# Second-product groups two by two, the seven products reordered, and a second PSUM buffer for X

## The chip, the cores and the metric

The kernel runs on one core of one Trainium2 chip. The metric is the time of one execution in microseconds on the device; the kernel before has a median of 1407.38 us over three runs (1406.71 to 1407.70). All arithmetic of the matmuls is done on a pair of reduced-precision float32 tiles, a high part and a low part (`hi`/`lo`, `xh`/`xl`, `hh`/`hl`), so every product of two matrices is three matmuls: high by high, high by low, low by high.

## The reference

Attention over local windows, then a mixture of eight experts with ReLU, then a layer with a rational activation. Only the middle part is touched here:

```python
P = np.exp(logits - logits.max())          # x @ w_gate, 1536 x 8
for _ in range(8):
    P /= P.sum(1, keepdims=True) + 1e-09
    P /= P.sum(0, keepdims=True) + 1e-09
    P *= N / E
for e in range(E):
    h = np.maximum(x @ w1[e], 0.0)         # 1536 x 512 by 512 x 1024
    ye = h @ w2[e]                         # 1024 x 512
    out += P[:, e:e + 1] * ye
```

## The kernel before, in words

The experts' hidden columns are cut into 16 units of 512. The first unit is worked out in the ordinary way, overlapped with the attention. The other 15 units are 30 subunits `v` of 256 columns, and each is done by `block(v, j)` for two halves `j` of the tokens (768 each): 60 blocks. A block forms the first product (weights 256 x 512 by 512 x 768 tokens) by Strassen's method in Winograd's form: seven products of quarters instead of eight, each of six matmuls of 384 columns (lines 1003 to 1005). The results are collected in three PSUM tiles: X (one bank, accumulated by four products in turn, and read after each of them), Y (two products) and Z (one product). `s1`, `s2`, `s3` are SBUF tiles: ScalarE copies X into one (lines 1018, 1023, 1029), VectorE adds Y or Z (lines 1026, 1032, 1039). `hidden` then makes the ReLU on ScalarE (`hh`, line 1011) and the low part on VectorE (`hl`, line 1012). That of `s2` is put off (`late`) until after product 0 of the next block.

The second product of a block is six groups of 128 tokens (`g2w`): each is six matmuls of 512 columns (lines 176 to 178) into one of three `psm` tiles, `p_v`, which VectorE then scales by the gate and adds to `accs` (line 1064; line 1059 for the first expert). The groups of a block are appended to the queue `g2q` after product 6, each due two ticks later, and issued in the next block.

The order is written out by hand: instructions go to each engine's queue in the order in which the Python code emits them, and each engine works its queue in order. Between the products stand the calls of `step`, here called places 0 to 5 of a block (after products 0, 1, 3, 4, 5, 6). `step` calls `tick`, which counts a point, may run one job, issues one group if the first in the queue is due, and from v = 2 on runs one of the `cv` jobs. The latter turn 64 pieces of the last layer's weights from float64 to float32 in five jobs each: a load by DMA (`cv_load`), `cv_round` (two VectorE instructions, then two on GpSimd, lines 782 to 789), `cv_join` (lines 795 and 798, which need GpSimd's result), `cv_add` (lines 803 and 806), and `cv_store` by DMA. The list `jobs` holds first the normalisation of P, due at points 4, 6, 8, ... 22: `sk_max_b`, `sk_first`, then eight `sk_step`s. Each `sk_step` is a matmul `csp <- cs` (line 738, column sums), VectorE's column scaling (lines 739 to 742) and, but for the last, row sums and the next `cs` (lines 730 to 734). The rule for jobs in `tick` is

```python
if g2q and g2q[0][0] <= point[0] or not g2q:
    run_job()
```

so a job waits while the first group in the queue is not yet due. At v = 0 the steps also run `rest`, the last two pieces of the token operands. After each product `sub_weights` gives GpSimd a piece of the next subunit's weights (at j = 0 `w_sums`, four sums of 128 x 256, lines 924 to 927; `w_op` and `w2_op`, lines 112 and 113, split into high and low), and SP the DMAs of the weights (`sa`, `sb`). SP also issues the `cv` loads and stores.

PSUM's eight banks in this stage: three for `psm`, one each for X, Y and Z (`psx`), two for `psb` (tag "g"), which holds the small tiles of the normalisation and is unused from v = 2 on.

Of the kernel before, what the change touches and what calls it, by code (L numbers as in the profile page):

```python
# [10 lines left out]
F32 = mybir.dt.float32  # L11
# [11 lines left out]
def kernel(  # L23
# [14 lines left out]
    nc = tc.nc  # L38
    B, H, S, D = q.shape
    NT, DM = out.shape  # L40
    NE, _, FE = w1.shape
    F2 = w_out.shape[0]
    P = 128
# [632 lines left out]
    psx = wctx.enter_context(tc.tile_pool(name="psx", bufs=1, space=PSUM))  # L676
    psb = wctx.enter_context(tc.tile_pool(name="psb", bufs=2, space=PSUM))
# [141 lines left out]
    point = [0]  # L819
    g2q = []  # L820

    def run_job():
        if jobs and jobs[0][0] <= point[0]:
            jobs.pop(0)[1]()

    def tick(cv=False):

        point[0] += 1
        if g2q and g2q[0][0] <= point[0] or not g2q:
            run_job()  # L830
        if g2q and g2q[0][0] <= point[0]:
            g2q.pop(0)[1]()
        if cv and cvjobs:
            cvjobs.pop(0)()

# [75 lines left out]

    wop = {}
    wS = {}
    OPS = ["A11", "S2", "A12", "S3", "S1", "A22", "S4"]

    def w_quarter(v, name):
        st = sg["v", v, 1]
        f, k = int(name[1]) - 1, int(name[2]) - 1
        return st[:, 2 * k:2 * k + 2, f * P:(f + 1) * P]
# [10 lines left out]
    def w_op(v, i):  # L930
        name = OPS[i]
        src = w_quarter(v, name) if name[0] == "A" else wS[v][:, int(name[1]) - 1]
        t = wpool.tile([P, 2, 2, P], F32R, tag="w1", name=f"w{name}_{v}")
        split(t[:, 0], t[:, 1], src, v == 0)
        wop[v, i] = t
# [8 lines left out]
    def sub_weights(v, j, i):  # L944

        n = v + 1
        if j == 0:
            if v == 0:
                if i < 2:
                    w2_op(0, i)  # L950
                elif i == 2:
                    dma_sub(1, 2)
                    w_sums(1)
                elif i != 4:
                    w_op(1, {3: 0, 5: 1, 6: 2}[i])
            elif n < NSUB:
                if i == 0:
                    w_sums(n)
                elif i % 2:
                    w_op(n, i // 2)  # L960
            elif i == 5:
                split_w(U1, 1, 0)
        elif n < NSUB:
            if i < 4:
                w_op(n, 3 + i)
            elif i < 6:
                w2_op(n, i - 4)
            if i == 3:
                dma_sub(n + 1, 1) if n + 1 < NSUB else dma_w(U1, 1, 0)
            if i == 5:  # L970
                dma_sub(n + 1, 2) if n + 1 < NSUB else dma_w(U1, 1, 1)
        else:
            if i in (0, 2, 4):
                split_w(U1, 1, 1 + i // 2)
            if i in (1, 5):
                dma_w(U1, 2, i // 4)

    late = []

    def step(v):  # L980
        tick(v > 1)
        if rest and point[0] % 2:
            rest.pop(0)()

    def block(v, j):

        n = NW
        o1, o2, ot = j * HT, j * HT + n, j * n
        X, Y, Z = (psx.tile([P, 512], F32, tag=t, name=f"{t}_{v}_{j}")[:, :n] for t in ("X", "Y", "Z"))
        s1, s2, s3 = (vpool.tile([P, n], F32, tag=t, name=f"{t}_{v}_{j}") for t in ("s1", "s2", "s3"))  # L990

        def xs(k, o):
            return lambda t: (xh[:, 2 * k + t, o:o + n], xl[:, 2 * k + t, o:o + n])

        def tt(i):
            return lambda t: (th[i][:, t, ot:ot + n], tl[i][:, t, ot:ot + n])

        def product(i, ps, get, start):
            w = wop[v, i]
            go = {} if start else {"skip_group_check": True}  # L1000
            for t in range(2):
                mh, ml = get(t)
                nc.tensor.matmul(ps, lhsT=w[:, 0, t], rhs=mh, start=start and t == 0, stop=False, **go)  # L1003
                nc.tensor.matmul(ps, lhsT=w[:, 0, t], rhs=ml, start=False, stop=False, **go)  # L1004
                nc.tensor.matmul(ps, lhsT=w[:, 1, t], rhs=mh, start=False, stop=t == 1, **go)  # L1005
            sub_weights(v, j, i)

        def hidden(c, half, src):
            hh = hp["pool"].tile([P, n], F32R, tag="hh", name=f"hh_v{v}_{j}_{c}{half}")
            hl = hp["pool"].tile([P, n], F32R, tag="hl", name=f"hl_v{v}_{j}_{c}{half}")  # L1010
            nc.scalar.activation(hh, src, AF.Relu)  # L1011
            nc.vector.scalar_tensor_tensor(  # L1012
                out=hl, in0=src, scalar=0.0, in1=hh.bitcast(F32), op0=ALU.max, op1=ALU.subtract
            )
            ht["v", v, j, c, half] = (hh, hl)

        product(0, X, xs(0, o1), True)
        nc.scalar.copy(s1, X)  # L1018
        while late:
            late.pop()()  # L1020
        step(v)
        product(1, X, tt(0), False)
        nc.scalar.copy(s2, X)
        step(v)
        product(2, Z, xs(1, o1), True)
        nc.vector.tensor_add(s1, s1, Z)  # L1026
        hidden(0, 0, s1)
        product(3, X, tt(1), False)
        nc.scalar.copy(s3, X)
        step(v)  # L1030
        product(4, Y, xs(0, o2), True)
        nc.vector.tensor_add(s3, s3, Y)  # L1032
        hidden(1, 1, s3)
        step(v)
        product(5, X, tt(2), False)
        hidden(1, 0, X)
        step(v)
        product(6, Y, xs(1, o2), False)
        nc.vector.tensor_add(s2, s2, Y)
        late.append(lambda: hidden(0, 1, s2))  # L1040
        for half in range(2):
            for t in range(n // P):
                g2q.append((point[0] + 2, lambda half=half, t=t: g2w(v, j, half, t)))
        step(v)

    def g2w(v, j, half, t):
        g = (j * HT + half * NW) // P + t
        u = UW + v // 2
        ps = psm.tile([P, 512], F32, tag="mm", name=f"p2_v{v}_{g}")
        o = t * P  # L1050

        def get(c):
            hh, hl = ht["v", v, j, c, half]
            return (hh[:, o:o + P], hl[:, o:o + P]), wt["v", v, c]

        mm3(ps, 2, get)
        a, e = acc[g], u // UPE
        if e == 0:
            nc.vector.tensor_add(a, a, ps)
        else:  # L1060
            if u == UPE and v % 2 == 0:
                assert not jobs
                acc_scale(g)
            nc.vector.scalar_tensor_tensor(  # L1064
                out=a, in0=ps, scalar=Pt[:, g, e:e + 1], in1=a, op0=ALU.mult, op1=ALU.add
            )
        if v == NSUB - 1:
            jobs.append((point[0] + 2, lambda: to_x(g)))

    def unit(u, blocks, delay, extra=None):  # L1070
        for b, (t0, n) in enumerate(blocks):
            for c in range(NCH):
                weights(u, b, len(blocks), c, True)
                g1(u, t0, n, c)
                weights(u, b, len(blocks), c, False)
                if c == NCH - 1:
                    for t in range(n // P):
                        g2q.append((point[0] + 2 + delay, lambda t0=t0, t=t: g2(u, t0, t)))
                tick()
                if extra:  # L1080
                    extra(b, c)
# [20 lines left out]
    for m in range(len(mains)):  # L1102
# [4 lines left out]
        if m == g1s - 1:  # L1107
            assert not plan
            for i in range(2, len(OPS)):
                w_op(0, i)  # L1110
# [3 lines left out]
    for v in range(NSUB):  # L1114
        for j in range(2):
            block(v, j)
    assert not cvjobs
    late.pop()()
    while g2q or jobs:
        tick()  # L1120
# [45 lines left out]
```

## Time and profile before

| | |
|---|---|
| median of three runs | 1407.38 us (1406.71 to 1407.70) |
| span of the profiled execution | 1408.2 us |
| TensorE matmuls busy | 1371.1 us (97%) |
| VectorE busy | 1083.5 us (77%) |
| GpSimd busy | 830.9 us (59%) |
| ScalarE busy | 503.9 us (36%) |
| mean granted TensorE clock | 0.995 |
| the 60 blocks | from 177 to 1125 us |

The profile is one execution of its own. Its span, first instruction to last, is 0.8 us above the median of the runs; no other time of that execution is listed. A busy TensorE is not TensorE at its peak: matmuls are pipelined, and the distance from the start of one matmul to the start of the next tells its cost better than the duration in its row. Of an engine that is not the bottleneck, idle time costs nothing by itself. A granted clock of 1.00 is 2.4 GHz, one of 0.5 is 1.2 GHz.

### The profile page before, as it was taken

To read this page: it belongs to the slowest core of one execution; us is meant where nothing else is said; L and a number is where in the kernel's file an instruction comes from. 1 tells how busy PE (TensorE), PEld (TensorE's weight loads), DVE (VectorE), ACT (ScalarE), POOL (GpSimd) and SP (SyncE) were. 2 spreads that over 40 slices of the span, in tenths; PEclk is the share of its full clock that TensorE was granted. 3 is DMA by queue.
4 is the path that set the end of the run, shared out by engine and by line. 5 is a ranking of instruction groups with operands and counts; after the bars stand their busy time and mean duration, and the time that the engine had idled before them with its cause. 6 is when DMAs were issued, how large, how long until landed. Compare 5 with 4: busy or idle time off the path is not lost.

```text
span 1408.2 us, 19502 instructions
## 1 busy us (share of the span) xinstructions
PE 1371.1 (97%) x7207; PEld 1209.2 (86%) x7207; DVE 1083.5 (77%) x1856; ACT 503.9 (36%) x1106; POOL 830.9 (59%) x1034
## 2 busy tenths in 40 slices
PE   6799989999999999999999999999999999999998
PEld 5788879988998989888988889888998888888886
DVE  6876867677777777676777777676777589999996
ACT  5665422321222222222222122112221268777673
POOL 5631584576767676676776776666776134545541
PEclk9999999999999999999999999999999999999999
DMA  9531021122112122122212122212221100100002
GB/s 240 141 99 29 0 60 38 54 64 64 60 57 77 55 79 64 55 62 64 64 53 79 54 78 64 64 54 64 64 69 62 39 31 15 46 30 31 31 7 83
DMA packets 90366, 86.08 MB, mean 61 GB/s; under 512 B 22944, under 2 KB 70048, under 8 KB 90272
## 3 DMA queue, kind: packets, MB, share of 16 engines
q1 hardware_dynamic: 90272, 84.84, 20.1%
q8 instruction: 57, 0.93, 0.3%
q14 instruction: 37, 0.30, 0.1%
HBM read 73.29 MB, written 11.53 MB: 60 GB/s over the span
## 4 chain that ended last, share of the span: by engine, by line
PE 62%; DVE 21%; POOL 7%; ACT 6%; DMA 2%; issue 1%; SPq 0%; ACTq 0%; DVEq 0%; POOLq 0%
PE p_v L178 10%; PE p_v L177 10%; PE p_v L176 10%; PE X L1003 5%; PE X L1004 5%; PE X L1005 5%; DVE r L216 4%; PE Y L1004 3%; PE Y L1005 2%; PE Y L1003 2%; DVE ta L219 2%; DVE ab L213 2%; DVE ab L202 2%; DVE ta L206 2%; DVE accs L248 1%; DVE ta L205 1%
## 5 line engine op out<-in xcount | busy, mean ns | idle before, releaser
L1064 DVE SCALAR_TENSOR_TENSOR accs<-p_v,Pt,accs 128x512 f32<-128x512 f32 x336 | 250.3, 745 | 71.9 <-PE p_v L178 70.6
L178 PE MATMUL p_v<-w2h_v,hl_v 128*128 128x512 f32 x720 | 286.3, 398 | 0.0
L177 PE MATMUL p_v<-w2l_v,hh_v 128*128 128x512 f32 x720 | 284.7, 395 | 0.0
L176 PE MATMUL p_v<-w2h_v,hh_v 128*128 128x512 f32 x720 | 282.1, 392 | 0.0
L1011 ACT ACTIVATE hh_v<-s 128x384 fp32r<-128x384 f32 x180 | 94.8, 527 | 349.5 <-DVE s L1026 198.9
L1012 DVE SCALAR_TENSOR_TENSOR hl_v<-s,hh_v 128x384 fp32r<-128x384 f32 x180 | 131.5, 730 | 104.5 <-ACT hh_v L1011 104.5
L788 POOL TENSOR_SCALAR ce<-ce 128x256 uint32<-128x256 uint32 x64 | 69.0, 1078 | 154.3 <-DVE ce L782 154.3
L178 PEld LDWEIGHTS p_v<-w2h_v,hl_v 128*128 128x128 f32 x720 | 135.2, 188 | 28.9
L176 PEld LDWEIGHTS p_v<-w2h_v,hh_v 128*128 128x128 f32 x720 | 135.6, 188 | 17.0
L177 PEld LDWEIGHTS p_v<-w2l_v,hh_v 128*128 128x128 f32 x720 | 135.3, 188 | 16.9
L223 POOL TENSOR_TENSOR hl<-ta,hh 128x512 fp32r<-128x512 f32 (+1 forms) x52 | 63.1, 1213 | 141.4 <-ACT hh L222 130.0
L1018 ACT COPY s<-X 128x384 f32<-128x384 f32 x60 | 28.7, 478 | 250.2 <-PE X L1005 250.2
L112 POOL TENSOR_SCALAR wS<-S 128x256 fp32r<-128x256 f32 x116 | 56.0, 483 | 89.3 <-PE X L1005 87.4
L176 PE MATMUL p<-xh,w1h 128*128 128x512 f32 (+2 forms) x288 | 102.8, 357 | 0.0
L113 POOL TENSOR_TENSOR wS<-S,wS 128x256 fp32r<-128x256 f32 x120 | 96.8, 807 | 9.7
L178 PE MATMUL p<-xh,w1l 128*128 128x512 f32 (+2 forms) x288 | 101.7, 353 | 0.0
L177 PE MATMUL p<-xl,w1h 128*128 128x512 f32 (+2 forms) x288 | 101.7, 353 | 0.0
L176 PE MATMUL p<-w2h,hh 128*128 128x512 f32 x240 | 95.2, 396 | 2.4 <-DVE accs L248 2.3
L178 PE MATMUL p<-w2h,hl 128*128 128x512 f32 x240 | 94.2, 393 | 1.8 <-DVE hl L191 1.7
L177 PE MATMUL p<-w2l,hh 128*128 128x512 f32 x240 | 94.0, 392 | 0.0
L113 POOL TENSOR_TENSOR w2l_v<-sb,w2h_v 128x512 fp32r<-128x512 f32 x60 | 80.5, 1341 | 5.0
L1003 PE MATMUL Y<-xh,wS 128*128 128x384 f32 x240 | 80.2, 334 | 2.4 <-DVE s L1032 2.4
(204 smaller groups left out, 3419.8 us busy)
## 6 DMA issues: line engine op xcount, KB each, us to landing
sa<-in_moe_w_dram SPq DMA_DIRECT2D x30, 512.0 KB, 3.5
sb<-in_moe_w_dram SPq DMA_DIRECT2D x30, 512.0 KB, 3.9
cv<-in_moe_w_in_dram SPq DMA_DIRECT2D x32, 256.0 KB, 3.5
cv<-in_moe_w_out_dram SPq DMA_DIRECT2D x32, 256.0 KB, 3.2
f_in<-cf SPq DMA_DIRECT2D x32, 128.0 KB, 2.2
f_out<-cf SPq DMA_DIRECT2D x32, 128.0 KB, 1.8
s<-f_in SPq DMA_DIRECT2D x8, 512.0 KB, 3.4
s<-f_out SPq DMA_DIRECT2D x8, 512.0 KB, 3.5
```

Of the source, the lines that this page charges most:

```text
L113: (sub or nc.gpsimd).tensor_sub(lo, src, hi.bitcast(F32))
L176: nc.tensor.matmul(ps, lhsT=sh, rhs=mh, start=(i == 0), stop=False)
L177: nc.tensor.matmul(ps, lhsT=sh, rhs=ml, start=False, stop=False)
L178: nc.tensor.matmul(ps, lhsT=sl, rhs=mh, start=False, stop=(i == n_k - 1))
L223: nc.gpsimd.tensor_sub(hl[:, :n], ta, hh[:, :n].bitcast(F32))
L788: nc.gpsimd.tensor_scalar(out=e, in0=e, scalar1=896, scalar2=0, op0=ALU.subtract, op1=ALU.max)
L1003: nc.tensor.matmul(ps, lhsT=w[:, 0, t], rhs=mh, start=start and t == 0, stop=False, **go)
L1004: nc.tensor.matmul(ps, lhsT=w[:, 0, t], rhs=ml, start=False, stop=False, **go)
L1005: nc.tensor.matmul(ps, lhsT=w[:, 1, t], rhs=mh, start=False, stop=t == 1, **go)
L1011: nc.scalar.activation(hh, src, AF.Relu)
L1012: nc.vector.scalar_tensor_tensor(out=hl, in0=src, scalar=0.0, in1=hh.bitcast(F32), op0=ALU.max, op1=ALU.subtract)
L1064: nc.vector.scalar_tensor_tensor(out=a, in0=ps, scalar=Pt[:, g, e:e + 1], in1=a, op0=ALU.mult, op1=ALU.add)
```

## The change

The seven products of a block come in another order, and so do the weight operands (`OPS`): S1 and S3 change places as well as A12 and S2. Products go to X, Z, X, Y, X, X, Y instead of X, X, Z, X, Y, X, Y. There are still six places in a block, now after products 0, 1, 2, 3, 4 and 6. `tick` takes a number of groups: two at the places 1, 3 and 4, none at 0, 2 and 5. From v = 2 on X comes from the two `psb` buffers. The sum and `hidden` of s1 now stand ahead of the copy of s2, and the sum of s3 directly behind the copy of s3.

```diff
-    def tick(cv=False):
+    def tick(cv=False, groups=1):
 
         point[0] += 1
         if g2q and g2q[0][0] <= point[0] or not g2q:
             run_job()
-        if g2q and g2q[0][0] <= point[0]:
-            g2q.pop(0)[1]()
+        for _ in range(groups):
+            if g2q and g2q[0][0] <= point[0]:
+                g2q.pop(0)[1]()
...
-    OPS = ["A11", "S2", "A12", "S3", "S1", "A22", "S4"]
+    OPS = ["A11", "A12", "S2", "S1", "S3", "A22", "S4"]
...
-    def step(v):
-        tick(v > 1)
+    def step(v, i):
+        tick(v > 1, 2 if i in (1, 3, 4) else 0)
...
-        X, Y, Z = (psx.tile([P, 512], F32, tag=t, name=f"{t}_{v}_{j}")[:, :n] for t in ("X", "Y", "Z"))
+        pools = (psb if v > 1 else psx, psx, psx)
+        X, Y, Z = (
+            p.tile([P, 512], F32, tag="g" if p is psb else t, name=f"{t}_{v}_{j}")[:, :n]
+            for p, t in zip(pools, ("X", "Y", "Z"))
+        )
...
-        step(v)
-        product(1, X, tt(0), False)
-        nc.scalar.copy(s2, X)
-        step(v)
-        product(2, Z, xs(1, o1), True)
+        step(v, 0)
+        product(1, Z, xs(1, o1), True)
         nc.vector.tensor_add(s1, s1, Z)
         hidden(0, 0, s1)
-        product(3, X, tt(1), False)
+        step(v, 1)
+        product(2, X, tt(0), False)
+        nc.scalar.copy(s2, X)
+        step(v, 2)
+        product(3, Y, xs(0, o2), True)
+        step(v, 3)
+        product(4, X, tt(1), False)
         nc.scalar.copy(s3, X)
-        step(v)
-        product(4, Y, xs(0, o2), True)
         nc.vector.tensor_add(s3, s3, Y)
         hidden(1, 1, s3)
-        step(v)
+        step(v, 4)
         product(5, X, tt(2), False)
         hidden(1, 0, X)
-        step(v)
         product(6, Y, xs(1, o2), False)
         nc.vector.tensor_add(s2, s2, Y)
         late.append(lambda: hidden(0, 1, s2))
         for half in range(2):
             for t in range(n // P):
                 g2q.append((point[0] + 2, lambda half=half, t=t: g2w(v, j, half, t)))
-        step(v)
+        step(v, 5)
```

## Rows read from the trace of the kernel before

**Rows 1.** Busy time by stretch; after the engines: granted clock, DMA share, GB/s.

```profile
68.70:72.20 3.50, 2.89 (x9) 2.53 (x10) 3.40 (x7) 1.77 (x5) 1.07 (x2) 0.51 0.69 183
188.20:195.10 6.90, 6.31 (x17) 5.30 (x18) 3.46 (x11) 1.28 (x3) 5.85 (x10) 0.51 0.10 37
...
300.00:1100.00 800.00, 796.05 (x3966) 714.12 (x3965) 586.45 (x1021) 167.23 (x357) 543.76 (x676) 1.00 0.21 64
```

**Rows 2.** Waits of TensorE's matmuls, 170 to 1125 us: total, times, longest.

```profile
PE X L1003 <- POOL wS L112: 4.4, 4, 1.4
PE Y L1003 <- DVE s L1032: 2.4, 1, 2.4
PE X L1003 <- DVE hl_v L1012: 0.7, 1, 0.7
PE X L1003 <- ACT s L1029: 0.6, 2, 0.3
PE X L1003 <- ACT s L1018: 0.6, 1, 0.6
```

**Rows 3.** Timelines of VectorE, ScalarE and TensorE around one late product 5.

```profile
434.02 0.29 DVE L782 TENSOR_SCALAR ce<-cv 128x256 uint32<-128x256 uint32 x1 [2.91 <-DMA cv<-in_moe_w_in_dram]
...
436.68 0.43 DVE L795 SCALAR_TENSOR_TENSOR cs<-cv,ce 128x256 uint32<-128x256 uint32 x1 [0.80 <-POOL ce L789]
...
440.36 0.54 DVE L1026 TENSOR_TENSOR s<-s,Z 128x384 f32<-128x384 f32 x1
...
440.94 0.52 ACT L1011 ACTIVATE hh_v<-s 128x384 fp32r<-128x384 f32 x1 [6.57 <-DVE s L1026]
441.37 0.46 ACT L1029 COPY s<-X 128x384 f32<-128x384 f32 x1
...
435.03 0.33 PE L1003 MATMUL Z<-xh,wA 128*128 128x384 f32 x1
...
436.07 0.33 PE L1003 MATMUL X<-th,wS 128*128 128x384 f32 x1
...
440.70 0.40 PE L178 MATMUL p_v<-w2h_v,hl_v 128*128 128x512 f32 x1
441.97 0.41 PE L1003 MATMUL X<-th,wA 128*128 128x384 f32 x1 [0.88 <-POOL wS L112]
```

**Rows 4.** Timeline of TensorE: the first matmuls of two blocks that follow each other.

```profile
241.16 0.33 PE L1003 MATMUL X<-xh,wA 128*128 128x384 f32 x1
...
256.80 0.33 PE L1003 MATMUL X<-xh,wA 128*128 128x384 f32 x1
```

**Rows 5.** Timelines: the normalisation's sums, and a block's start.

```profile
203.68 0.16 DVE L739 TENSOR_SCALAR cr<-csp 128x8 f32<-128x8 f32 x1
...
206.58 0.34 DVE L734 TENSOR_REDUCE cs<-Pt 128x8 f32<-128x96 f32 x1
...
220.25 0.16 DVE L739 TENSOR_SCALAR cr<-csp 128x8 f32<-128x8 f32 x1
...
222.23 0.36 DVE L734 TENSOR_REDUCE cs<-Pt 128x8 f32<-128x96 f32 x1
...
225.01 0.34 PE L1003 MATMUL X<-xh,wA 128*128 128x384 f32 x1
...
226.71 0.53 ACT L1011 ACTIVATE hh_v<-s 128x384 fp32r<-128x384 f32 x1
...
228.51 0.28 PE L738 MATMUL csp<-cs,ones 128*128 128x8 f32 x2
...
228.83 0.17 DVE L739 TENSOR_SCALAR cr<-csp 128x8 f32<-128x8 f32 x1 [0.15 <-PE csp L738]
```

**Rows 6.** Groups of instructions, 300 to 1130 us: busy, mean ns, idle before them.

```profile
L1064 DVE SCALAR_TENSOR_TENSOR accs<-p_v,Pt,accs 128x512 f32<-128x512 f32 x317 | 236.1, 745 | 69.7 <-PE p_v L178 69.0
...
L924 POOL TENSOR_TENSOR S<-sa 128x256 f32<-128x256 f32 x25 | 22.8, 912 | 0.8
```

**Rows 7.** Timeline of TensorE ahead of the half-clock stretch at 68.7 us.

```profile
66.06 0.70 PE L456 MATMUL sc<-accs,qz 128*128 128x120 f32 x4 [1.49 <-DVE a L463]
```

## The prediction

> **What bounds the kernel now.** I read the windows first: from 300 to 1100 us TensorE is busy 796.05 of 800 us at the full clock, VectorE 586 and GpSimd 544 [rows 1]. So in the long middle the sixty blocks go at TensorE's own pace, and another engine counts only where TensorE waits for it. The timeline gives that pace: a first product took 1.04 us (435.03 to 436.07) [rows 3], and a block 15.64 us (241.16 to 256.80) [rows 4], so a group takes (15.64 - 7 x 1.04) / 6 = 1.39 us. The change leaves out and adds no matmul; it can only move waits. The list of what TensorE waited for, 170 to 1125 us, is therefore the whole budget [rows 2]:
> - 3.7 us in block 0: 2.4 for the sum s3 += Y, 0.7 for the second reader of X, 0.6 for the copy s1.
> - 4.4 + 0.6 = 5.0 us in six waits of product 5 (writes X, L1003), once in ten blocks. The timeline shows one: the group's last matmul starts at 440.70 and would be over at 440.93; product 5 starts at 441.97, 1.04 us late where the row shows 0.88 [rows 3]. With 0.16 more on each, the six cost 6.0 us.
>
> A third loss stands in no list of waits: from 188.2 to 195.1 us, right behind block 0's waits, the granted clock is 0.51, which is the 1.2 GHz level [rows 1]. 6.9 us at half pace, less 0.7 us of waiting within, cost about 3 us.
>
> **The six waits of product 5: minus 6.0 us.** In the one shown, the releaser named is GpSimd, but its weights were not what was late: VectorE waited 2.91 us for a cv load, so s1 += Z began at 440.36; ScalarE's ReLU of s1 at 440.94; behind it in ScalarE's queue the copy of s3 at 441.37, which product 5 needs [rows 3]. Z was complete at 436.07, so the sum was 3.9 us late. In the new order Z is product 1 (its end: 2.1 us into a block), the copy behind the ReLU is that of s2, and the product that needs it is number 4, at 9.7 us (two products, two groups, two products, two groups: 4 x 1.04 + 4 x 1.39). With the sum 3.9 us late it begins at 6.4, the ReLU ends near 7.0 and the copy near 7.5: 2 us to spare. Product 5 now needs only the s3 copy, with two groups (2.78 us) for a 0.46 us copy. I take the whole 6.0; the lower bound is 5.0, as listed.
>
> **New waits from block 4 on: plus 1 us.** What is late next is s3 += Y, for product 6 at 14.6 us. The cv jobs still come one at a place, but between places 1 and 2 VectorE now has no other work, so a join that follows its round there must wait for GpSimd. In the instance of before, the round's start, GpSimd's two steps and the join's start took 434.02 to 436.68 = 2.66 us, and from the join to the sum behind it, with one group's addition between, 3.68 us [rows 3]. In the new order the second group's product is complete at 4.9 us, so the round starts near 6.1; join at 8.8; 3.68 us and one more addition of 0.745 us [rows 6] later, at 13.2, s3 += Y starts, and ends at 13.8. That leaves 0.8 us. This meeting comes in one block of five (five cv jobs against six places), 11 times. Were GpSimd first to finish the four weight sums of a new subunit (0.91 us each [rows 6], 3.6 us), which stand in every second block, product 6 would wait about 2 us in some 5 of these: plus 10. The sums of before were over before the round came, so I take 1 us; bounds 0 and 10. DMAs: SP's order is kept, except that cv's store and load of place 4 now pass ahead of the sb load issued at product 5, which spares them its wait; the price is nothing where the sb load's tile is used a block later. PSUM: two groups in a row need two of three psm buffers; the additions are 0.745 us against 1.39 a group, so none is short.
>
> **The second buffer of X: nothing from block 4 on, plus 0.5 us before.** Up to v = 1 X keeps one buffer, and product 0 now follows product 5 after one product (1.04 us), where a group, a product and a group lay. ReLU and subtraction of X take about 0.3 + 0.5 + 0.55 us: some 0.25 us late at two borders. Bounds 0 and 1.
>
> **Block 0: minus 0.7 us.** No group is due there, so products stand back to back, and its 3.7 us of waits [rows 2] only change places: the s2 copy now stands behind the ReLU of s1, the s3 copy behind a cast of the last operands. What sets the block's end is in both orders VectorE's chain: the last operands, s3 += Y, the two subtractions. I give it the last of the waits, 0.7; bounds minus 1.5 and plus 1.
>
> **The row and column sums: plus 9.6 us.** This is what the diff doesn't show. A job runs in a tick only when the first group in the queue is due (or none is queued). Until now the queue's old last group was still due at place 5. With two groups at places 1, 3 and 4 the queue is empty before place 5; the six new ones are appended there, due two ticks on. So place 5 runs no job, and the jobs due at points 6, 12 and 18 run at 7, 13 and 19, place 0 of blocks 1 to 3. The next ones, due at 8, 14 and 20, run at place 1: only product 1 (1.04 us) lies between. Each job's matmul csp needs cs from the job ahead, and stands in TensorE's queue ahead of the groups.
> How long cs takes: cr starts 0.32 us after csp (228.51, 228.83), and from cr to the end of cs VectorE takes 2.34 us (220.25 to 222.59) up to 3.24 us (203.68 to 206.92) [rows 5]. Ahead of it in VectorE's queue stands now hl of the former block's s2, whose ReLU starts 1.70 us after product 0 starts (225.01, 226.71) and takes 0.53 us [rows 5]; hl takes 0.5 more, so cr starts at 2.7 us and cs ends at 5.1 to 6.0. TensorE stands ready at 2.2 us: a wait of 2.9 to 3.8 us, 3.3 in the middle. For the pair at 13 and 14 and that at 19 and 20, that is 6.6. At points 7 and 8 the first job is sk_first (a copy, an exponential, a row sum): I give that pair a little less, 3.0. Sum 9.6; above 11.4, below 3 x 1.5 = 4.5, were hl not ahead. Until now at least a group and a product lay between two jobs, and TensorE waited nowhere.
> The Trainium skill ("SBUF — State Buffer", "Who interferes with whom") says that VectorE instructions with two SBUF inputs, or in a two-port mode, are held up by GpSimd; 2.34 against 3.24 us for the same nine instructions agrees, and by it GpSimd's weight splitting would make each of the three waits one of 3.8, 11.4 in all.
>
> **The clock: plus 1.5 us.** Another half-clock stretch, 68.7 to 72.2 us [rows 1], follows a wait of 1.49 us at 66.06 [rows 7] and lasts 3.5 us. A wait of 3.3 us is longer than the 2.4 of block 0. I take three stretches of the short kind (half of 3.5 lost, less what falls into waiting: 1.5 each) in place of the one that costs 3. Bounds: none (minus 3) and the long kind behind each wait (3 x 3 - 3 = plus 6).
>
> **Sum.** -6.0 + 1 + 0.5 - 0.7 + 9.6 + 1.5 = +5.9 us. The profiled span is 1408.2, 0.8 above the median of the runs; on the median 1407.4 + 5.9 = 1413.3. A measurement of this kernel tells 0.2% (2.8 us) from no change.
>
> **Rivals.**
> - *Faster: the pairs of sums cost little.* If cs comes when hl isn't ahead (1.5 us each) and no half-clock stretch remains: -6.0 - 0.7 + 4.5 + 0.5 - 3 = -4.7, 1402.7. With those 3 us of clock back and the other terms as in the sum, it decides from waits of under 1.8 us each (-6.0 + 1 + 0.5 - 0.7 - 3 + 3 x 1.8 = -2.8). For it: the six waits surely go. Against: hl is issued ahead of the job in the text of the block. 0.25, of which 0.15 below 1404.6 and 0.10 within 0.2%.
> - *The clock falls for long at every wait:* plus 6 instead of 1.5: 1417.8. For it: 6.9 us behind block 0's waits. Against: the stretch at 68.7 us is half as long. The Trainium skill ("TensorE: Matmul & The Clock Gate", "HAM oscillation") speaks against a change that makes TensorE idle between bursts: each idle stretch brings the low clock again. That the low clock follows waits, the trace shows; by the rule the time is this rival's. 0.15.
> - *GpSimd holds up the sums of every fifth block:* plus 10 instead of 1, 1422.3. For it: no vector work between places 1 and 2. Against: GpSimd is busy 68% only [rows 1]. 0.10.
> - The forecast, 1409 to 1417: 0.50, of which 0.08 within 0.2%, where block 0 and the clock come out well.
>
> Faster 0.15, same 0.18, slower 0.67. The range 1403 to 1421 leaves out the lower part of the first rival and the upper part of the third; with both signs possible, the forecast's own is 1409 to 1417.
>
> **What would show it.** TensorE's waits list csp for cs three times, about 3 us each, between 188 and 230 us; product 5 of X is gone from it after 240 us; a block in the middle still takes 15.6 us; the half-clock stretches can be counted. It is wrong if the csp waits are under 2 us, if no wait of block 4 on has gone, or if product 6 waits for s3 += Y in every fifth block.

## The result and the profile after

The changed kernel takes 1416.07 us (median of five runs, 1414.81 to 1418.03) against 1407.38 us before: 1.0060 times the time, 95% interval 1.0050 to 1.0071. Its profiled execution has a span of 1416.3 us against 1408.2, 8.1 us more. This execution took 1418.03 us, the slowest of the five: wherever the span and the time of one execution are both listed, the time is 1.7 us longer. By that the profiled execution of before took some 1409.9 us, 2.5 above its median, and not 0.8 as its span alone suggests. The page's first part shows the same number of matmuls and 7.5 us more of busy TensorE; ScalarE is busy 7.6 us more too, still 36% of the span:

```profile
span 1416.3 us, 19561 instructions
...
PE 1378.6 (97%) x7207; PEld 1216.9 (86%) x7207; DVE 1083.2 (76%) x1856; ACT 511.5 (36%) x1106; POOL 829.6 (59%) x1034
```

Where the 8.1 us lie is read from the starts of the blocks ("from start to start" means from the start of one matmul to that of another). The timeline of TensorE gives the first matmul of blocks 0, 4, 5 and 59; of the kernel after:

```profile
177.26 0.33 PE L1008 MATMUL X<-xh,wA 128*128 128x384 f32 x1
...
254.21 0.33 PE L1008 MATMUL X<-xh,wA 128*128 128x384 f32 x1
...
269.85 0.33 PE L1008 MATMUL X<-xh,wA 128*128 128x384 f32 x1
...
1115.41 0.33 PE L1008 MATMUL X<-xh,wA 128*128 128x384 f32 x1
```

and of the kernel before, where block 4 starts at 241.16 [rows 4]:

```profile
176.95 0.33 PE L1003 MATMUL X<-xh,wA 128*128 128x384 f32 x1
...
1107.87 0.33 PE L1003 MATMUL X<-xh,wA 128*128 128x384 f32 x1
```

| stretch | before | after | difference |
|---|---|---|---|
| up to block 0 | 176.95 | 177.26 | +0.3 |
| blocks 0 to 3 | 64.21 | 76.95 | +12.7 |
| blocks 4 to 58 | 866.71 | 861.20 | -5.5 |
| block 59 and the rest | 300.33 | 300.89 | +0.6 |

A block of the middle takes 15.64 us (254.21 to 269.85), as before [rows 4]; 55 such are 860.2. So the middle (blocks 4 to 58) now takes 1.0 us more than that where it took 6.5 more, and four blocks at the start lose more than that gains.

The list of TensorE's waits after, 170 to 1140 us, answers to [rows 2]:

```profile
PE csp L738 <- DVE cs L734: 8.6, 3, 3.1
PE X L1008 <- ACT s L1037: 1.3, 1, 1.3
PE X L1008 <- DVE hl_v L1017: 1.0, 2, 0.7
```

The six waits of product 5 are gone; asked for 254 to 1120 us alone, the list is empty (the 1.3 us are product 5 of block 0, which starts at 184.12). In their place stand three waits of the matmul csp. One of them in the timelines of TensorE, ScalarE and VectorE (block 2), which answers to [rows 5]:

```profile
210.11 0.41 PE L1008 MATMUL X<-xh,wA 128*128 128x384 f32 x1 [0.28 <-DVE hl_v L1017]
...
212.33 0.34 PE L1010 MATMUL Z<-xh,wA 128*128 128x384 f32 x1
215.77 0.51 PE L738 MATMUL csp<-cs,ones 128*128 128x8 f32 x2 [3.10 <-DVE cs L734]
...
211.87 0.53 ACT L1016 ACTIVATE hh_v<-s 128x384 fp32r<-128x384 f32 x1
...
212.43 1.07 DVE L1017 SCALAR_TENSOR_TENSOR hl_v<-s,hh_v 128x384 fp32r<-128x384 f32 x1 [2.00 <-ACT hh_v L1016]
213.43 0.15 DVE L739 TENSOR_SCALAR cr<-csp 128x8 f32<-128x8 f32 x1
...
215.40 0.32 DVE L734 TENSOR_REDUCE cs<-Pt 128x8 f32<-128x96 f32 x1
```

What to see here is the order on VectorE: it is idle for 2.00 us until the ReLU of s2 is done, then makes hl, and only then cr, although csp was ready at 211.5; cs ends at 215.72, 5.6 us after the block's start, and TensorE, ready since 212.5, goes on at 215.77.

The windows show what follows each wait, granted clock behind the engines, and the middle for comparison; they answer to [rows 1]:

```profile
192.00:198.80 6.80, 6.00 (x15) 4.84 (x16) 4.83 (x15) 0.52 (x1) 3.94 (x7) 0.50 0.02 4
215.90:219.30 3.40, 3.40 (x10) 2.72 (x11) 2.48 (x11) 0.52 (x1) 0.00 (x0) 0.50 0.00 0
236.40:243.20 6.80, 5.70 (x14) 4.56 (x15) 4.50 (x16) 0.52 (x1) 0.00 (x0) 0.50 0.00 0
300.00:1100.00 800.00, 800.00 (x3988) 720.64 (x3987) 592.33 (x1032) 174.04 (x358) 553.10 (x688) 1.00 0.21 65
```

Behind each of the three csp waits TensorE runs at 1.2 GHz for 3.4 or 6.8 us; it is busy there for 15.1 us, half of which, an estimated 7.5 us, are lost. Before, one such stretch with 6.31 us of busy time lost 3.2.

How long these stretches are differs from one execution to another. The kernel with one buffer for X (below) has the same code in blocks 0 to 3; its csp waits are 2.44, 2.69 and 3.14 us long, and behind them the clock is low for 3.4, 3.4 and 6.8 us:

```profile
192.80:196.20 3.40, 3.40 (x10) 2.72 (x9) 3.12 (x12) 0.00 (x0) 1.73 (x3) 0.50 0.01 2
213.30:216.70 3.40, 3.40 (x10) 2.63 (x9) 2.75 (x11) 0.34 (x1) 0.00 (x0) 0.50 0.00 0
233.80:240.60 6.80, 6.29 (x16) 5.13 (x17) 4.32 (x15) 0.52 (x1) 0.00 (x0) 0.50 0.00 0
```

A first wait of 2.42 us was followed by 6.8 us in one execution, and one of 2.44 us by 3.4 us in the other.

### The profile page after: what moved, and what is told of

It is laid out like the page before. It is cut to its first block, busy times and chain, and to the rows that moved or that the text cites. A ratio compares the mean times of both kernels' runs of the same rounds, so it can differ in the third digit from the quotient of the medians.

```text
span 1416.3 us, 19561 instructions
## 1 busy us (share of the span) xinstructions
PE 1378.6 (97%) x7207; PEld 1216.9 (86%) x7207; DVE 1083.2 (76%) x1856; ACT 511.5 (36%) x1106; POOL 829.6 (59%) x1034
## 4 chain that ended last, share of the span: by engine, by line
PE 71%; DVE 21%; ACT 6%; issue 1%; DMA 1%; SPq 0%; POOL 0%; ACTq 0%; DVEq 0%; POOLq 0%
PE p_v L177 12%; PE p_v L178 12%; PE p_v L176 12%; PE X L1008 6%; PE X L1010 6%; PE X L1009 6%; DVE r L216 4%; PE Y L1010 3%; PE Y L1008 3%; PE Y L1009 3%; DVE ta L219 2%; DVE ab L213 2%; DVE ab L202 2%; DVE ta L206 2%; PE Z L1010 1%; PE Z L1009 1%
## 5 line engine op out<-in xcount | busy, mean ns | idle before, releaser
L1069 DVE SCALAR_TENSOR_TENSOR accs<-p_v,Pt,accs 128x512 f32<-128x512 f32 x336 | 239.0, 742 | 40.0 <-PE p_v L178 39.5
L113 POOL TENSOR_TENSOR wS<-S,wS 128x256 fp32r<-128x256 f32 x120 | 91.3, 761 | 11.0 <-ACT wS L110 1.3
L1010 PE MATMUL X<-th,wS 128*128 128x384 f32 x240 | 81.7, 341 | 0.0
L1008 PE MATMUL X<-th,wS 128*128 128x384 f32 x240 | 81.7, 340 | 0.0
```

Of the source, the lines that this page charges most:

```text
L113: (sub or nc.gpsimd).tensor_sub(lo, src, hi.bitcast(F32))
L1069: nc.vector.scalar_tensor_tensor(out=a, in0=ps, scalar=Pt[:, g, e:e + 1], in1=a, op0=ALU.mult, op1=ALU.add)
```

## The experiments

Ratios are those to the kernel before, timed beside each, with their 95% intervals.

**Sums apart.** The changed kernel; only the jobs' points are moved, so that groups lie between any two sums.

```diff
-    jobs += [(8 + 2 * i, lambda i=i: sk_step(i == 7)) for i in range(8)]
+    jobs += [(p, lambda i=i: sk_step(i == 7)) for i, p in enumerate((10, 11, 14, 16, 17, 20, 22, 23))]
```

> The changed kernel with the jobs' points alone moved: the eight row and column sums are due at points 10, 11, 14, 16, 17, 20, 22, 23 (places 3, 4, 1, 3, 4, 1, 3, 4 of blocks 1 to 3), so that at least two groups lie between two of them. My theory (the 8.7 us come from sums that stand one product apart, 9.1 us of waiting from start to start, and from the half-clock stretches behind these waits, some 4 to 7 us): 1400 to 1403 us, and csp is gone from TensorE's waits. Rival (the sums are work of VectorE that TensorE must wait for somewhere in these four blocks): the wait turns up at another tile, 1412 to 1416 us.

Measured: 1407.9 us, ratio 1.0002 (0.9991 to 1.0014). That is 0.6% less than the changed kernel and no better than the one before; neither theory gave this time. Blocks 0 to 3 take 68.9 us in its profile, against 76.95 after and 64.21 before. The waits of TensorE, 170 to 1150 us:

```profile
PE X L1008 <- DVE hl_v L1017: 3.9, 2, 2.8
PE X L1008 <- ACT s L1037: 1.6, 1, 1.6
...
PE csp L738 <- DVE cs L734: 0.5, 1, 0.5
```

The csp wait is gone but for 0.5 us, and part of the lost time has come back at product 0. The timeline of VectorE around 206 us, with TensorE's product 0, shows how:

```profile
204.76 0.32 DVE L734 TENSOR_REDUCE cs<-Pt 128x8 f32<-128x96 f32 x1
205.00 1.27 DVE L1064 TENSOR_TENSOR accs<-accs,p_v 128x512 f32<-128x512 f32 x2
206.19 0.55 DVE L1017 SCALAR_TENSOR_TENSOR hl_v<-X,hh_v 128x384 fp32r<-128x384 f32 x1
...
206.89 0.41 PE L1008 MATMUL X<-xh,wA 128*128 128x384 f32 x1 [2.76 <-DVE hl_v L1017]
```

A sum at place 4 stands ahead of two groups' additions and of the subtraction of X, and while X has one buffer product 0 waits for that. So distance on TensorE is not all: the sum must not stand ahead of the next thing that TensorE needs.

**At most two sums in a block.** The next step from that: sums at places 1 and 3 only, spread to block 5.

```diff
-    jobs += [(8 + 2 * i, lambda i=i: sk_step(i == 7)) for i in range(8)]
+    jobs += [(p, lambda i=i: sk_step(i == 7)) for i, p in enumerate((10, 14, 16, 20, 22, 26, 28, 32))]
...
-        pools = (psb if v > 1 else psx, psx, psx)
+        pools = (psb if v > 2 else psx, psx, psx)
```

> The changed kernel with at most two of the normalisation's sums in a block, due at points 10, 14, 16, 20, 22, 26, 28, 32 (places 3 and 1), none at place 4, where a sum in the first experiment stood ahead of the subtraction of X; X has its second buffer from v = 3 on. My theory (the groups two by two cost nothing by themselves; it is the place of the sums): 1400 to 1403 us, product 0 waits under 0.5 us at a border. Rival (groups two by two cost in these blocks wherever the sums stand, since with X in one buffer VectorE is late for product 0): 1405 to 1410 us.

Measured: 1405.5 us, ratio 0.9977 (0.9966 to 0.9989). In its profile blocks 0 to 3, with five of the eight sums in them, take 60.2 us, where the changed kernel took 76.95 and the one before 64.21; product 0 waits for 0.7 us at most at the borders between blocks. Then block 4 takes 20.1 us where 15.64 is usual: cv work has begun there, VectorE waits for GpSimd with a join, the sum stands behind the join, TensorE waits for the additions that free a psm buffer, and behind that wait the clock is low again for 3.4 us:

```profile
PE p_v L176 <- DVE accs L1064: 2.0, 1, 2.0
...
PE X L1008 <- DVE hl_v L1017: 1.3, 3, 0.7
```

The time is the rival's, and not mine, and a border waits for 0.7 us where I allowed 0.5. The rival's reason is not what the trace shows, though: with two sums a block and no cv work, groups two by two cost these four blocks nothing, and what is lost is lost in block 4, where sums meet cv work. That meeting neither theory had.

**One group at each place.** The changed kernel, its two by two undone, order of products and second buffer kept.

```diff
-        tick(v > 1, 2 if i in (1, 3, 4) else 0)
+        tick(v > 1)
```

> The changed kernel with one group at each of the six places in place of two at three; order of products and second buffer of X as changed. My theory: with a group due at every place the jobs run at even points again, the csp waits go, and the six waits of product 5 stay away, since they hung on the order alone: 1400 to 1403 us. Rival (the new order of products needs its groups two by two, else the s3 copy and s3 += Y come late for products 5 and 6): 0.3 us or more in each block, 1416 us or more.

Measured: 1400.06 us, ratio 0.9952 (0.9939 to 0.9965). This is the version that beats both kernels. Its profiled execution is the fastest of its five (1397.85 us). Its block 4 and its block 59 start at

```profile
235.13 0.33 PE L1008 MATMUL X<-xh,wA 128*128 128x384 f32 x1
...
1095.68 0.33 PE L1008 MATMUL X<-xh,wA 128*128 128x384 f32 x1
```

so the middle takes 860.55 us, 0.4 above 55 times 15.64, and its list of waits between 235 and 1100 us is empty. Blocks 0 to 3 take 61.7 us. Of the list between 170 and 1150 us one row is left of the sums:

```profile
PE csp L738 <- DVE cs L734: 1.1, 1, 1.1
```

This wait is not one that the change brought: the two kernels below that keep the old order of products, copy first and two buffers for X, have one of 1.1 us at the same job. So the two by two is what costs, by where it puts the sums, and in the middle it brings nothing: 861.20 against 860.55 us.

**Waits filled.** The changed kernel with dummy work where TensorE waits; what it writes is not used.

```diff
+    def fill():
+        ps = psb.tile([P, 512], F32, tag="g", name="fill")
+        for _ in range(17):
+            nc.tensor.matmul(ps[:, 0:NW], lhsT=xh[:, 0, 0:P], rhs=xh[:, 0, 0:NW], start=True, stop=True)
...
-    def sk_step(last):
+    def sk_step(last, i):
+        if i in (0, 3, 6):
+            fill()
         sk_col()
...
-    jobs += [(8 + 2 * i, lambda i=i: sk_step(i == 7)) for i in range(8)]
+    jobs += [(8 + 2 * i, lambda i=i: sk_step(i == 7, i)) for i in range(8)]
```

> The changed kernel with 17 matmuls of 384 columns put ahead of the csp matmul at points 8, 14 and 20; what they write is not used. They take about 17 x 0.173 = 2.9 us, where TensorE waits 2.4 to 3.1 us. My theory: the waits are filled but not shortened, so that only the clock changes: the three half-clock stretches between 190 and 245 us, which cost 6.9 us, stay away or mostly so: 1409 to 1412 us. Rival (the half-clock stretches cost nothing of their own, or come anyway): 1416 us.

Measured: 1410.35 us, ratio 1.0024 (1.0012 to 1.0036). The windows show no low clock where there were three stretches of it:

```profile
190.00:197.00 7.00, 7.00 (x39) 6.49 (x38) 5.57 (x17) 1.11 (x3) 5.47 (x10) 1.00 0.01 4
197.00:230.00 33.00, 32.58 (x170) 29.34 (x169) 23.21 (x62) 6.05 (x13) 14.57 (x21) 1.00 0.11 32
230.00:250.00 20.00, 19.78 (x102) 17.70 (x101) 13.59 (x35) 3.61 (x8) 10.95 (x15) 1.00 0.22 66
```

The kernel issues 51 matmuls more and is 0.36% (1.0060 less 1.0024), some 5 us, faster than the changed one. In the two profiles blocks 0 to 3 take 69.9 us for 76.95, 7.1 less. That is the price of the low clock, apart from the waits themselves, which are only filled.

**Copy first.** The kernel before, with the s3 copy emitted ahead of the sum and the ReLU of s1.

```diff
         product(2, Z, xs(1, o1), True)
-        nc.vector.tensor_add(s1, s1, Z)
-        hidden(0, 0, s1)
         product(3, X, tt(1), False)
         nc.scalar.copy(s3, X)
+        nc.vector.tensor_add(s1, s1, Z)
+        hidden(0, 0, s1)
```

> The kernel before with one thing moved: the copy of s3 from X is emitted ahead of s1 += Z and its ReLU, so that it no longer stands behind this ReLU in ScalarE's queue. My theory of the six waits of product 5 (5.0 us in the list, 6.0 from start to start): they go, 1401 to 1402.5 us. Rival (product 5 waits for its weights from GpSimd, which the list names as the releaser in four of the six): 1407.4 us and the waits stay.

Measured: 1404.12 us, ratio 0.9973 (0.9963 to 0.9984). All six waits are gone: the list of TensorE's waits between 240 and 1120 us, where [rows 2] has 5.0 us, is empty, and blocks 4 to 58 take 860.6 us for 866.7. The weights from GpSimd, named as the releaser in four of the six, were not what was late: in the trace of before, product 5 starts 0.14 to 0.15 us after the end of the s3 copy in all six. The time fell by 3.7 us where some 5 to 6 were expected, though the middle gave 6.1 in the one profile. One likely reason is that the six waits are not always as long: the kernel with two buffers for X, below, has the old order too, and its middle lost 3.8 us where the profile of before lost 6.5. With 3.8 the measured 3.7 would fit. Whether the execution makes this difference or the buffer, no run was made to show.

**One buffer for X.** The changed kernel with `pools = (psx, psx, psx)`.

> The changed kernel with one PSUM buffer for X throughout. My theory: with products 5, 6 and 0 back to back, product 0 of every block waits for the subtraction that still reads X, 0.3 to 0.45 us as at the two borders ahead of v = 2, more in the blocks that have cv work at place 4: 56 times that is 17 to 40 us, so 1433 to 1456 us. Rival (the second buffer does nothing, TensorE's order leaves time enough): 1416 us.

Measured: 1451.2 us, ratio 1.0300 (1.0280 to 1.0319). Every block of the middle takes 16.0 to 17.3 us. The rows of its list between 252 and 1150 us:

```profile
PE X L1008 <- DVE hl_v L1017: 9.3, 22, 1.1
PE X L1008 <- POOL S L926: 6.9, 5, 1.4
```

In the changed order the second buffer is worth 2.4%, some 34 us.

**Two buffers for X in the kernel before.** The same two `psb` buffers from v = 2 on, nothing else of the change.

> The kernel before with the second buffer of X from v = 2 on and nothing else. My theory: product 0 never waited for X there after block 0 (no such row in the list of waits), so the time stays: 1407.4 us, within 1.5. Rival (the gain of the one-by-one kernel comes in part from the second buffer, for instance by fewer semaphore waits): 1402 to 1405 us.

Measured: 1408.95 us, ratio 0.9996 (0.9987 to 1.0005). Nothing, as product 0 never waited there. Its trace has the waits of product 5 at the same six places as before, each beginning again 0.14 to 0.15 us after the s3 copy, but shorter; blocks 4 to 58 take 864.0 us. The rows between 240 and 1120 us (one of the six is too short to be listed):

```profile
PE X L1007 <- ACT s L1033: 1.3, 4, 0.6
PE X L1007 <- POOL wS L112: 0.9, 1, 0.9
```

**One by one, one buffer.** The order of the products alone is left of the change.

> The changed kernel with one group at each of six places and one buffer for X throughout, so of the change only the order of the products is left. My theory: product 6 and a group (2.4 us) lie between product 5 and the next product 0, enough for ReLU and subtraction of X (some 1.5 us): 1400 to 1403 us as with two buffers. Rival (VectorE's queue delays the subtraction in the blocks with cv work): 1405 us or more, with product 0 in TensorE's waits.

Measured: 1408.25 us, ratio 0.9994 (0.9985 to 1.0002). My theory fell and its rival held. The list between 238 and 1120 us:

```profile
PE X L1008 <- POOL w2h_v L112: 2.2, 5, 0.4
PE X L1008 <- DVE hl_v L1017: 2.0, 5, 0.4
```

At two borders in each ten blocks product 0 waits for the subtraction of X: in all ten cases of the list it starts 0.14 to 0.15 us after that subtraction ends, whichever engine the row names. At five of them a join stands ahead of the subtraction in VectorE's queue, at the other five the two instructions of `cv_add`. The timeline of VectorE ahead of a border of the first kind shows the join's second instruction at 1.40 us, where it took 0.50 at another place:

```profile
286.63 0.50 DVE L798 TENSOR_TENSOR cm<-cm,cs 128x256 uint32<-128x256 uint32 x1
...
299.48 1.40 DVE L798 TENSOR_TENSOR cm<-cm,cs 128x256 uint32<-128x256 uint32 x1
300.80 0.54 DVE L1017 SCALAR_TENSOR_TENSOR hl_v<-X,hh_v 128x384 fp32r<-128x384 f32 x1
```

Blocks 4 to 58 take 867.1 us. With one buffer the new order gives back at product 0 what it gained at product 5; with two it keeps it: 1400.06 us.

## Why the prediction was right, step by step

The forecast was 1413.3 us, slower, for the reason that it gave; 1416.07 is 2.8 us beyond it. The two main terms, six waits gone and three csp waits come, were right in cause and place. The sizes of two smaller ones agree less well, and one agrees by luck.

- *The six waits, -6.0, and new waits, +1.* The middle gained 5.5 us: it had lost 6.5 and still loses 1.0. The copy-first kernel shows the cause that was argued for the six: ScalarE's copy behind a ReLU that waits for VectorE. The margin at product 6 held; that product does not appear in the waits. So the +1 was hit by luck: what is left is 0.20 us in one block of ten, between two matmuls of a group (0.35 and 0.31 us from start to start, for 0.23) where the profile names no wait, and its cause is open. The size of the six was read from one execution, which was 2.5 us above the median; the kernel with two buffers for X lost only 3.8 us to them.
- *The sums, +9.6.* 8.6 us in the list, in three waits of up to 3.1, at blocks 1, 2 and 3, and 9.1 us from start to start with the 0.16 each that the list leaves out. The 3.8 us for each wait, given as what GpSimd could make of it, did not come. The chain was the one described: ReLU of s2, hl, cr to cs. One detail was wrong: in block 0 no old group is queued, so the job due at point 6 ran at 7 before the change as well (its matmul stands at 191.01 us there, in block 1). For that pair what is new is only that no group lies between the two jobs. That the sums' places are the cause is shown: with one group a place, or with two sums a block, the waits of 2.4 to 3.1 us go. What the forecast did not ask is whether other places in the same blocks would be free: in the first of the experiments blocks 0 to 3 still took 4.7 us more than before.
- *The second buffer, nothing and +0.5.* 0.45 and 0.30 us at the two borders, from start to start. That it is needed at all in the changed order (34 us) the forecast did not work out, since it asked only for the change as it was made.
- *Block 0, -0.7.* It takes 10.2 us where it took 11.8: -1.6, just past the bound of -1.5.
- *The clock, +1.5.* In the profiled executions this term was too small. The forecast took three short stretches; one was short and two long, and they lost 7.5 us where before 3.2 were lost: +4.4. With -1.6, 9.1, 0.75 and 4.4 the four blocks come to 12.65 us, and 12.7 were measured. The rival of the long stretch behind every wait was nearer than the forecast in this term (+6) and in the time (1417.8). But the profiled execution is the slowest of five, with a mean granted clock of 0.990; that of the median run is 0.992, which over 1416 us is an estimated 3 us less lost, and the kernel with one buffer for X had one long stretch behind the same three waits. So how many stretches are long is not decided by the waits alone, and neither the forecast's count nor the rival's is shown to be the usual one. The filled kernel shows that the loss is one of its own.
- *Not forecast:* 0.6 us behind block 59 and 0.3 ahead of block 0. Every kernel here with groups two by two takes 300.9 us from block 59 on, and every one with single groups 300.3 to 300.4, so the first belongs to the two by two. The second is less than executions differ there: block 0 starts between 173.4 and 177.4 us in the ten traces.
- *The rival of GpSimd holding up the sums of every fifth block* did not come: the list of waits is empty in the middle. The faster rival, waits under 1.8 us each, fell with the 2.4 to 3.1 of the profile.

## What to carry to other kernels

When work is issued from a queue at fixed places, look at what else hangs on the queue's state: here a job's turn depended on whether a group was due, and emptying the queue early moved serial jobs next to each other. A chain that goes from one engine to another and back needs other work of its length between its links on the waiting engine, and must not stand ahead of the next thing that engine needs on the other. An accumulator that is read several times can stand in one buffer as long as enough other work lies between the last product that is read and the next first product (a second buffer changed nothing measurable in the old order and 2.4% in the new one); reorder, and that has to be worked out again. And a list of waits is that of one execution: the six waits cost 6.5 us in the trace of before and 3.8 in that of a kernel that differs from it only in a buffer which gained nothing.

## What the runs showed of the hardware

TensorE's clock fell to 1.2 GHz behind each of three waits of 2.4 to 3.1 us, for 3.4 or 6.8 us; the same waits filled with 2.9 us of matmuls left it at 2.4 GHz, and a kernel with more work was 5 us faster for it. The wait alone does not tell the length: 2.42 us were followed by 6.8 us at 1.2 GHz in one execution, 2.44 us by 3.4 us in another. The Trainium skill ("TensorE: Matmul & The Clock Gate", "Part 1: The HAM clock gate") says that activity releases the throttle and that there are just two levels; the granted clocks of 0.50 and 1.00 agree.

A VectorE instruction of one kernel took 0.50 us at one place and 1.40 at another, on operands of the same shape and type. "SBUF — State Buffer" of the Trainium skill ("Who interferes with whom") names GpSimd's reads as what holds up VectorE instructions with two SBUF inputs; no run here was made to tell that from another cause.
